# Gate and up with seven half products instead of eight in three of seven tile pairs, and the inverse transform token by token

## The chip, the cores and the metric

The program runs on one core of a Trainium2 chip. A core has TensorE (PE, with the weight load PEld shown apart), VectorE (DVE), ScalarE (ACT), GpSimd (POOL) and SyncE (SP), which here issues all DMAs. Each engine works through its instructions in the order in which the kernel emits them, and waits for the others through semaphores. The metric is the time of one execution on the device, in microseconds; lower is better.

## The reference

8192 tokens of 448 channels go through two blocks with a modulated layer norm each. The first is a Fourier transform over the tokens, a small two-layer network per frequency, and the inverse transform. The second is a gated feed-forward network of 1792 hidden channels:

```python
mod = (_silu(c) @ w_mod).reshape(c.shape[0], 6, 1, -1)
h = _layernorm(x, axis=-1) * (1 + ca) + sa
x = x + ga * _A_ref(h, A_w1, A_b1, A_w2, A_b2)
h = _layernorm(x, axis=-1) * (1 + cb) + sb
x = x + gb * (_gelu(h @ w_gate) * (h @ w_up)) @ w_down
```

Inputs and outputs are float32. The kernel keeps that accuracy by splitting operands into a high and a low float16 part and summing three products: high by high, high by low, low by high.

## The kernel before

**Stages.** A forward transform, the network on frequencies and the first half of the inverse transform take about 370 us. Then the second half of the inverse and the feed-forward network run over 32 chunks (`nch`) of 256 tokens, two blocks of 128 (called "tokens" b=0, 1 below). This loop over chunks `i` is the part that the change touches.

**Gate and up.** The 1792 hidden channels are 14 tiles of 128. They go in seven pairs t=0..6: q=0 is hidden tile t, q=1 is tile t+7. A step k=2t+q of the loop (`gate_up(i, k)`, L1096) computes gate (pr=0) and up (pr=1) of one hidden tile for the 256 tokens into one PSUM bank `pgu`: for each of the two, ten matmuls of 256 columns (L1087). The 448 channels are three whole k-tiles (each wh by high, wh by low, wl by high) and a last one of 64 channels, where high and low stand above each other. What is left of that last one, wl by high, is done for two neighbouring units (i, t) together by eight matmuls of 64 rows (L1116), when the first unit of the pair (`first_pair`, (7i+t) even) has ended its q=1. So a first unit's two outputs leave PSUM after its q=1; a second unit's leave after each q. With t even, the unit is first of its pair in even chunks and second in odd ones.

**The way out of a tile.** `gate_up_out` (L1120): ACT takes the gelu of the gate (L1123), DVE multiplies by up (L1128) into the tile `x` (three buffers), and after q=1 POOL forms four sums of 128x128 blocks (L1134 to L1137), with which `down` needs seven products instead of eight. One unit later, after odd k, `quantize` (L1139) writes the seven blocks as high (ACT, L1145) and low part (DVE, L1146).

**Down.** After k=2 of the next chunk `down(i-1)` (L1158) does seven products of 21 matmuls. The first two end in `b1` (a "pd" bank) and `b2` (a "pc" bank); ACT copies p1 (L1176) out of `b1`, the next product uses the other "pd" bank, and the one after it the bank that the p1 copy has freed.

**Beside it**, hooks prepare the chunk after next, i+2: at k=3 `split_g` and `split_v` split the transform matrix g and the values v (high on ACT L105, low on POOL L107), for both tokens; at k=6 `inverse` (six float32r matmuls, L987 to L989); at k=7 `residual` (L998, L999), at k=8 to k=10 the statistics and the inverse root, at k=11 and 12 `norm2` (L1036, L1037) into a tile of its own, at k=13 `pack_hi` (ACT, L1042) and `pack_lo` (POOL). At k=0 of the following chunk 16 DMA transposes bring the packed rows to `nt`, the moving operand of gate and up. Loads of v, g and xx (the input rows) of chunk i+2 are issued at k=0.

Of the kernel before, what the change touches and what calls it, by code (L numbers as in the profile page):

```python
# [37 lines left out]
NTT = len(PKO)  # L38
LAM = 0.01
# [6 lines left out]
def spectral_geglu(ctx, tc, x, w1, b1, w2, b2, wg, wu, wd, cvec, wmod, cf1, cs2, cmi, cgm, out):  # L46
# [272 lines left out]
    with ExitStack() as bctx:  # L319
# [359 lines left out]
        def row_scales():  # L679
# [8 lines left out]
            pow2(sk, bnd)  # L688
# [50 lines left out]
        def scales1():  # L739
# [20 lines left out]
            pow2(sw, mxa)  # L760
# [122 lines left out]
        def load_g(i):  # L883
            g = ep.tile([128, CB, 128], F32, tag="g", name="g")
            dma(g, cgm[:, i * CB : (i + 1) * CB, :])
            xx = ep.tile([128, CB, D], F32, tag="xx", name="xx")
            dma(xx, xv[:, i * CB : (i + 1) * CB, :])
            nxt.setdefault(i, {}).update({"g": g, "xx": xx})
# [22 lines left out]

        def split_g(i):
            gh = ep.tile([128, CB, 128], F32R, tag="gh", name="gh")
            gl = ep.tile([128, CB, 128], F32R, tag="gl", name="gl")
            split(gh, gl, nxt[i]["g"], el=G)
            nxt[i]["g"] = gh, gl
# [32 lines left out]
    with ExitStack() as cctx:  # L949
# [7 lines left out]

        def load_d8(t):
            load_d(t, *(cp2.tile([128, n, HC], F32, tag=f"dr{n}", name="dr", bufs=2) for n in (3, 4)))
# [8 lines left out]
        def split_v(i, cs=slice(0, D)):  # L968
            n = nxt[i]
            if "vh" not in n:  # L970
                n["vh"] = cp.tile([128, CB, D], F32R, tag="vh", name="vh")
                n["vl"] = cp.tile([128, CB, D], F32R, tag="vl", name="vl")
            for b in each(i):
                split(n["vh"][:, b, cs], n["vl"][:, b, cs], n["v"][:, b, cs], el=G)

        def inverse(i, cs=slice(0, D), tag="pc"):
            nxt[i]["ps"] = []
            for b in range(CB):
                ps = bank(tag, "pi2")[:, cs]
                if i < 3:  # L980

                    T.matmul(ps, nxt[i]["g"][:, b], nxt[i]["v"][:, b, cs], start=True, stop=True)
                    nxt[i]["ps"].append(ps)
                    continue
                vh, vl = nxt[i]["vh"], nxt[i]["vl"]
                gh, gl = nxt[i]["g"]
                T.matmul(ps, gh[:, b], vh[:, b, cs], start=True, stop=False)  # L987
                T.matmul(ps, gl[:, b], vh[:, b, cs], start=False, stop=False)  # L988
                T.matmul(ps, gh[:, b], vl[:, b, cs], start=False, stop=True)  # L989
                nxt[i]["ps"].append(ps)  # L990

        def residual(i, cs=slice(0, D)):
# [383 lines left out]
```

## Time and profile before

| | us |
|---|---|
| runs shown, median (lowest, highest) | 1941.23 (1938.67, 1942.99) |
| the profiled execution, time | 1942.27 |
| the profiled execution, span in the trace | 1940.5 |
| mean granted TensorE clock | 0.995 of full |

The page gives each engine's busy time as a share of the span; the chain that ended last names, going back from the end, what each step waited for. The windows view cuts a stretch of time out and gives the same busy times for it, with the clock and the DMA share. The timeline lists instructions in order of time, neighbours of one kind merged ("x7"): start, duration from the first start to the last end, engine, line, and in brackets how long the engine was idle before and what released it. A matmul's duration holds its way through the array, so the pace of a row of matmuls is read from start to start, not from one duration.

### The profile page before, as it was taken

How to read it: one execution, taken by the hardware profiler on the slowest of the kernel's cores; microseconds unless marked ns; L12 is line 12 of the kernel's file. 1: busy time of each engine (PE TensorE's matmuls, PEld its weight loads, DVE VectorE, ACT ScalarE, POOL GpSimd, SP SyncE). 2: the span in 40 equal slices, each digit the busy share in tenths (PEclk: the TensorE clock that was granted, in tenths of full speed). 3: DMA queues.
4: the chain of work that ended last, by engine and by line, in shares of the span. 5: the costliest groups of instructions: out<-in, count | busy, mean ns of one | idle time of the engine just before them, and what ended most of it. 6: DMA issues, size and time to landing. Idle time of an engine off the chain costs nothing.

```text
span 1940.5 us, 43566 instructions
## 1 busy us (share of the span) xinstructions
PE 1901.1 (98%) x17636; PEld 1694.6 (87%) x17636; DVE 1108.7 (57%) x2352; ACT 790.1 (41%) x1342; POOL 1157.7 (60%) x1466
## 2 busy tenths in 40 slices
PE   7899999899999999999999999999999999999998
PEld 3599999778888888888888888888888888888897
DVE  8677788786555555555555555555555555555533
ACT  5587888553333333333333333333333333333322
POOL 3157655256666666666666666666666666666644
PEclk9899999999999999999999999999999999999999
DMA  9999777541111111111111111111111111111000
GB/s 351 313 286 261 194 195 196 166 125 48 44 44 44 43 43 43 43 43 44 43 44 43 43 44 43 44 44 42 45 43 44 44 43 44 43 44 44 21 16 20
DMA packets 167330, 163.35 MB, mean 84 GB/s; under 512 B 87252, under 2 KB 145496, under 8 KB 167128
## 3 DMA queue, kind: packets, MB, share of 16 engines
q1 hardware_dynamic: 167128, 160.57, 28.3%
q8 instruction: 138, 2.26, 0.5%
q14 instruction: 64, 0.52, 0.1%
HBM read 97.44 MB, written 47.25 MB: 75 GB/s over the span
## 4 chain that ended last, share of the span: by engine, by line
PE 86%; DVE 4%; ACT 3%; issue 3%; DMA 2%; POOL 1%; SPq 1%; ACTq 0%; POOLq 0%; DVEq 0%
PE pgu L1087 53%; PE pdn L1155 8%; PE pdn L1153 8%; PE pdn L1154 8%; PE ps L202 2%; DVE y L463 2%; PE pi L989 1%; PE pi L988 1%; PE pi L987 1%; POOL yl L107 1%; DVE st L163 1%; ACT th L105 0%; DMA raw<-in_B_w_gate 0%; POOL tl L107 0%; ACT zh L376 0%
## 5 line engine op out<-in xcount | busy, mean ns | idle before, releaser
L1087 PE MATMUL pgu<-nt,wh 128*128 128x256 f16 x6272 | 834.2, 273 | 0.1
L1087 PEld LDWEIGHTS <-wh 128*128 128x128 f16 x6272 | 602.7, 98 | 98.5 <-issue 31.0
L1123 ACT ACTIVATE gel<-pgu,dg 128x256 f32<-128x256 f32 x448 | 200.3, 473 | 793.2 <-PE pgu L1087 756.1
L1087 PE MATMUL pgu<-nt,wl 128*128 128x256 f16 (+1 forms) x3584 | 501.3, 272 | 0.6 <-DVE x L1128 0.6
L1155 PE MATMUL pdn<-wd,ac 128*128 128x224 f16 x1568 | 406.1, 259 | 0.2 <-DVE ac L1146 0.2
L1153 PE MATMUL pdn<-wd,ac 128*128 128x224 f16 x1568 | 406.1, 259 | 0.0
L1154 PE MATMUL pdn<-wd,ac 128*128 128x224 f16 x1568 | 406.1, 259 | 0.0
L1134 POOL TENSOR_TENSOR x<-x 128x128 f32<-128x128 f32 x223 | 239.9, 1076 | 264.0 <-DVE x L1128 230.5
L1146 DVE SCALAR_TENSOR_TENSOR ac<-x,sa_act,ac 128x896 f16<-128x896 f32 (+1 forms) x225 | 308.2, 1370 | 81.9 <-ACT ac L1145 81.9
L1087 PEld LDWEIGHTS <-wl 128*128 128x128 f16 (+1 forms) x3584 | 297.8, 97 | 57.6 <-issue 24.4
L1128 DVE TENSOR_TENSOR x<-pgu,gel 128x256 f32<-128x256 f32 x448 | 179.6, 418 | 278.7 <-ACT gel L1123 278.0
L1145 ACT ACTIVATE ac<-x,sa_act 128x896 f16<-128x896 f32 (+1 forms) x225 | 232.9, 1035 | 46.5 <-POOL x L1137 44.5
L1190 POOL TENSOR_TENSOR o<-u,p 128x224 f32<-128x224 f32 x32 | 21.0, 657 | 291.6 <-DVE u L1189 291.6
L1135 POOL TENSOR_TENSOR x<-x 128x128 f32<-128x128 f32 x223 | 158.1, 709 | 17.5
L1155 PEld LDWEIGHTS <-ac 128*128 128x128 f16 x1568 | 153.4, 98 | 0.5 <-DVE ac L1146 0.5
L1154 PEld LDWEIGHTS <-ac 128*128 128x128 f16 x1568 | 153.4, 98 | 0.4
L1153 PEld LDWEIGHTS <-ac 128*128 128x128 f16 x1568 | 153.4, 98 | 0.4
L107 POOL TENSOR_TENSOR yl<-y,yh 128x448 fp32r<-128x448 f32 x63 | 78.9, 1252 | 75.6 <-ACT yh L105 63.0
L463 DVE SCALAR_TENSOR_TENSOR y<-pm,t 64x224 f32<-64x224 f32 x256 | 99.5, 389 | 41.3 <-ACT t L455 37.4
L1136 POOL TENSOR_TENSOR x<-x 128x128 f32<-128x128 f32 x223 | 113.0, 507 | 0.0
L1137 POOL TENSOR_TENSOR x<-x 128x128 f32<-128x128 f32 x223 | 109.2, 490 | 0.0
L107 POOL TENSOR_TENSOR tl<-tr,th 128x896 f16<-128x896 f32 x30 | 57.3, 1909 | 69.5 <-DMA tr<-td 38.2
(281 smaller groups left out, 2728.4 us busy)
## 6 DMA issues: line engine op xcount, KB each, us to landing
tr<-td SPq DMA_DIRECT2D x64, 224.0 KB, 4.3
vd<-us SPq DMA_DIRECT2D x64, 224.0 KB, 3.3
xx<-in_A_x SPq DMA_DIRECT2D x32, 448.0 KB, 3.3
v<-vd SPq DMA_DIRECT2D x63, 224.0 KB, 2.7
out<-x SPq DMA_DIRECT2D x31, 448.0 KB, 2.6
xt<-in_A_x SPq DMA_DIRECT2D x15, 896.0 KB, 14.8
td<-xt SPq DMA_DIRECT2D x48, 224.0 KB, 4.3
nt<-pk SPq DMA_TRANSPOSE x480, 2.3
```

The lines of the kernel that those rows point to most:

```text
L107: (el or V).tensor_tensor(lo, src, h, ALU.subtract)
L463: V.scalar_tensor_tensor(y[ri * 64 : ri * 64 + 64, gi], pv[si, ri], LAM, tv[si, ri], op0=ALU.add, op1=ALU.min)
L1087: T.matmul(pgu[i, t, q][:, pr * H : (pr + 1) * H], w[rows, tw, f0 : f0 + 128], nts[i][rows, tn, :], start=start, stop=stop, skip_group_che ...
L1123: S.activation(gl, ps[:, :H], AF.Gelu_apprx_tanh, scale=dg)
L1128: V.tensor_tensor(dst, ps[:, H : 2 * H].rearrange("p (b c) -> p b c", b=2), gl.rearrange("p (b c) -> p b c", b=2), ALU.mult)
L1134: e.tensor_tensor(s1, a21, a22, ALU.add)
L1135: e.tensor_tensor(s2, s1, a11, ALU.subtract)
L1145: S.activation(ac[:, 0, k], x[:, k], AF.Copy, scale=sc)
L1146: V.scalar_tensor_tensor(ac[:, 1, k], x[:, k], sc, ac[:, 0, k], op0=ALU.mult, op1=ALU.subtract)
L1153: T.matmul(ps, ac[:, 0, ka], wds[t][:, 0, kb], start=t == 0, stop=False)
L1154: T.matmul(ps, ac[:, 0, ka], wds[t][:, 1, kb], start=False, stop=False)
L1155: T.matmul(ps, ac[:, 1, ka], wds[t][:, 0, kb], start=False, stop=t == NP - 1)
```

## The change

Of the 448 channels, the first 256 (k-tiles 0 and 1) form a 2x2 grid of blocks with the two tokens on one side and, with the two hidden tiles t and t+7, on the other. Eight products of 128-blocks are replaced by seven (Winograd's form), for t = 0, 2 and 4, from chunk 3, 4 and 5 on (`SP`). Each product is gate and up times three matmuls of 128 columns. The other 192 channels stay (`rest`, from k-tile 2).

- PE: `gate_up_s1` (q=0) does six of the products, with three intermediate sums x, of which each is copied from PSUM to SBUF (`u`) by ACT before the next product is added onto it. A seventh bank user, `px` ("pc"), holds x and one product y. `gate_up_s2` (q=1) does the last product. `gate_up_out` adds u (and y) to the outputs on DVE: one 512-column add for q=0, two for q=1.
- The token side needs four sums of blocks for each chunk: `s_sums` (POOL) and `s_pack` (ACT, POOL) at k=2 for chunk i+1, and `s_transposes` at k=3, eight more DMA transposes into a longer `nt`.
- The weight side needs sums of blocks once: `sp_load`, `sp_sums`, `sp_round`, in chunks 2 to 4.
- To make room, `norm2` writes into the tile `xx`, `load_xx` moves to k=3, g and v are split one token at a time (b=0 at k=2 ahead of `down`, b=1 at k=5), and `inverse1` runs per token at k=5 and k=7, with the residual at k=6 and k=8.
- The scales for gate and up and for the normalised rows become smaller by a factor of four (`pow2(..., 13)`).

```diff
+SP = {0: 3, 2: 4, 4: 5}
...
+        def split_v(i, b):
             n = nxt[i]
+            for key, w in (("g", 128), ("v", D)):
+                h, l = (cp.tile([128, w], F32R, tag=key + p, name=key + p) for p in "hl")
+                split(h, l, n[key][:, b], el=G)
+                n[key + "2"] = h, l
...
+        def inverse1(i, b):
+            ps = bank("pc", "pi2")[:, :D]
+            (gh, gl), (vh, vl) = nxt[i]["g2"], nxt[i]["v2"]
+            T.matmul(ps, gh, vh, start=True, stop=False)
+            T.matmul(ps, gl, vh, start=False, stop=False)
+            T.matmul(ps, gh, vl, start=False, stop=True)
...
+        def s_sums(i):
+            n = nxt[i]["n"]
+            a11, a12, a21, a22 = (n[:, b, k * 128 : (k + 1) * 128] for b in range(2) for k in range(2))
+            s = nxt[i]["s"] = x8()
+            G.tensor_tensor(s[:, 0], a21, a22, ALU.add)
+            G.tensor_tensor(s[:, 1], s[:, 0], a11, ALU.subtract)
+            G.tensor_tensor(s[:, 2], a11, a21, ALU.subtract)
+            G.tensor_tensor(s[:, 3], a12, s[:, 1], ALU.subtract)
+
+        def s_pack(i):
+            s = nxt[i]["s"]
+            ps = nxt[i]["ps16"] = cp.tile([128, 4, 2, 128], F16, tag="pks", name="pks")
+            S.copy(ps[:, :, 0], s[:, :4])
+            G.tensor_tensor(ps[:, :, 1], s[:, :4], ps[:, :, 0], ALU.subtract)
...
+        def rest(i, t, q, pr, first_pair, j0):
+            seq = [(wh, j, j) for j in range(j0, 4)] + [(wh, j, j + 5) for j in range(j0, 3)] + [(wl, j, j) for j in range(j0, 3)]
+            for j, (w, tw, tn) in enumerate(seq):
+                last = not first_pair and not j0 and j == len(seq) - 1
+                gu(i, t, q, pr, w, full, tw, tn, first_pair and pr == 0 and j == 0, last)
...
+        def sp_product(i, t, o, ka, kb, start=False, stop=False):
...
+            for pr in range(2):
+                for n, (l, la) in enumerate(((0, 0), (0, 1), (1, 0))):
+                    T.matmul(
+                        o[:, pr],
+                        weight(pr, l),
+                        act(la),
...
+        def gate_up_s1(i, t, first_pair):
+            pv = bank("pc", "px").rearrange("p (x r c) -> p x r c", x=2, r=2)
+            sums["px"] = pv
+            x, u = pv[:, 0], sums["u"]
+            sp_product(i, t, x, 0, 0, start=True)
+            sp_product(i, t, pv[:, 1], 3, 3)
+            S.copy(u[:, :, 0], x)
+            rest(i, t, 0, 0, first_pair, 2)
+            sp_product(i, t, x, 4, 6)
+            S.copy(u[:, :, 1], x)
+            rest(i, t, 0, 1, first_pair, 2)
+            o = outs(i, t, 0)
+            sp_product(i, t, o[:, :, 0], 1, 1, stop=not first_pair)
+            sp_product(i, t, x, 5, 4, stop=True)
+            S.copy(u[:, :, 2], x)
+            sp_product(i, t, o[:, :, 1], 2, 5, stop=not first_pair)
+
+        def gate_up_s2(i, t, first_pair):
+            for pr in range(2):
+                rest(i, t, 1, pr, first_pair, 2)
+            sp_product(i, t, outs(i, t, 1)[:, :, 0], 6, 2, stop=not first_pair)
...
         def gate_up_out(i, t, q):
+            if seven(i, t):
+                u, o = sums["u"], outs(i, t, q)
+                if q == 0:
+                    V.tensor_tensor(o, o, u[:, :, 0::2], ALU.add)
+                else:
+                    y = sums["px"][:, 1].unsqueeze(2).broadcast_to([128, 2, 2, 128])
+                    V.tensor_tensor(u[:, :, 1:3], y, u[:, :, 1:3], ALU.add)
+                    V.tensor_tensor(o, o, u[:, :, 1:3], ALU.add)
...
-            3: [(2, split_g), (2, split_v)],
-            6: [(2, inverse)],
-            7: [(2, residual)],
-            8: [(2, stats2)],
+            3: [(2, load_xx), (1, s_transposes)],
+            5: [(2, inverse1, 0), (2, split_v, 1)],
+            6: [(2, residual, slice(0, D), [0])],
+            7: [(2, inverse1, 1)],
+            8: [(2, residual, slice(0, D), [1]), (2, stats2)],
...
+                if k == 2 and 3 <= i + 1 < nch:
+                    s_sums(i + 1)
+                    s_pack(i + 1)
+                if k == (4, 3, 2)[min(i, 2)] and 3 <= i + 2 < nch:
+                    split_v(i + 2, 0)
+                for fn, *args in sp_work.pop(i * NFT + k, []):
+                    fn(*args)
                 if k == 2 and i > 0:
                     down(i - 1)
```

`quantize` after odd k, `pack_hi` and `pack_lo` at k=13 and `down` at k=2 keep their places in the loop.

More of the change, by code (lines that the diff above doesn't have):

```diff
@@ L995, in residual @@
             x1 = x1t[i][:, :, cs]
-            for b in range(CB):
+            for b in bs:
                 e = V if i < 3 else G
@@ L1103, in gate_up @@
                         pgu[(*divmod(u, NP), qq)] = bank(tag, "pgu")
[L1104 to L1107 removed]
+            if seven(i, t):
+                (gate_up_s1, gate_up_s2)[q](i, t, first_pair)
+            else:
+                for pr in range(2):
+                    rest(i, t, q, pr, first_pair, 0)
             if not first_pair:
@@ L1268, in spectral_geglu @@
         pack_lo(0)
+        load_g(1)
         for t0 in range(0, 7, 2):
```

121 lines of the change are left out of this document (86 added, 35 removed).

## The prediction

> **What bounds the kernel now.** I read the page's busy shares first, then the chain that ended last, then two neighbouring chunks in the windows view.
>
> ```profile
> PE 1901.1 (98%) x17636; PEld 1694.6 (87%) x17636; DVE 1108.7 (57%) x2352; ACT 790.1 (41%) x1342; POOL 1157.7 (60%) x1466
> ...
> PE 86%; DVE 4%; ACT 3%; issue 3%; DMA 2%; POOL 1%; SPq 1%; ACTq 0%; POOLq 0%; DVEq 0%
> ```
>
> ```profile
> 861.62:910.24 48.62, 48.62 (x467) 43.27 (x465) 25.85 (x52) 15.45 (x26) 31.75 (x42) 1.00 0.16 43
> 910.24:958.12 47.88, 47.88 (x460) 43.08 (x458) 24.49 (x50) 15.97 (x27) 30.50 (x40) 1.00 0.16 44
> ```
>
> The windows are chunk 10 (even) and chunk 11 (odd), cut where their first tile starts on PE. The columns are length, then PE, PEld, DVE, ACT, POOL busy, clock, DMA. PE is busy in all of both, so in a chunk the time is PE's own work: less PE work is worth its full length, and any wait that PE gets is paid in full. ACT works 16 of 48 us, so it has time; whether it has it at the right moment is the question of this change.
>
> **The matmuls.** I write k for a half tile (k = 2t+q), T0 for the moment when PE starts the half tile spoken of.
>
> ```profile
> 861.62 0.93 PE L1087 MATMUL pgu<-nt,wh 128*128 128x256 f16 x7
> 862.38 0.49 PE L1087 MATMUL pgu<-nt,wl 128*128 128x256 f16 x3
> 862.71 0.93 PE L1087 MATMUL pgu<-nt,wh 128*128 128x256 f16 x7
> ```
>
> ```profile
> 250.84 0.22 PE L368 MATMUL ps<-s,th 128*112 128x128 f16 x1
> ...
> 252.13 0.22 PE L370 MATMUL ps<-s,tl 128*112 128x128 f16 x1
> ```
>
> ```profile
> 416.62 0.40 PE L1069 MATMUL ptr<-ident,pk 128*128 128x128 f16 x4
> ```
>
> Ten matmuls of 256 columns take 1.09 us from start to start, 0.109 each. The second fence holds the first and the last of 24 matmuls of 128 columns, each with a weight load of its own (112 columns): 1.29/23 = 0.056 us. The third has the change's shape exactly, but only four of it: (0.40 - 0.22)/3 = 0.060. A seven-product unit drops 24 matmuls of 256 columns (2.62 us) and adds 7 x 2 x 3 = 42 of 128 (2.35 at 0.056, 2.52 at 0.060). It saves 0.26 to 0.10 us; I take 0.26, from the longer run. There are 29 + 28 + 27 = 84 such units: 22 us, and no more.
>
> One rule speaks against even that. The Trainium skill, "TensorE: Matmul & The Clock Gate", section "Back-to-back issue gap", gives about 81 ns for a sustained stream of weight load and 128-column matmul; the rows above, 56 ns over 24 pairs, do not agree, and by 81 ns a unit would cost 0.78 us more than before instead of 0.26 less.
>
> **The first copy.** `gate_up_s1` puts product 1 and the product kept as y on PE (12 x 0.056), then four matmuls of 256 (0.44): after 1.11 us PE wants to add the next product onto x, and must not before ACT has copied x to u. The copy is queued on ACT behind everything emitted for the half tile before.
>
> ```profile
> 885.09 0.93 PE L1087 MATMUL pgu<-nt,wh 128*128 128x256 f16 x7
> ...
> 885.29 0.47 ACT L1123 ACTIVATE gel<-pgu,dg 128x256 f32<-128x256 f32 x1 [9.89 <-PE pgu L1087]
> 885.66 1.03 ACT L1145 ACTIVATE ac<-x,sa_act 128x896 f16<-128x896 f32 x1
> ...
> 933.71 0.94 PE L1087 MATMUL pgu<-nt,wh 128*128 128x256 f16 x7
> ...
> 934.43 1.04 ACT L1145 ACTIVATE ac<-x,sa_act 128x896 f16<-128x896 f32 x1
> ```
>
> These are k=4 of chunk 10 and of chunk 11, PE's start and ACT's work. The gelu of k=3 can only run once PE has ended k=3, that is after T0, and the quantize of an odd half tile stands right behind it. It ends 886.69 - 885.09 = 1.60 us after T0 in the even chunk, 1.76 in the odd one. None of this is touched by the change. The copy itself, 256 columns out of PSUM, is not in the trace; its nearest rows are these two:
>
> ```profile
> L1123 ACT ACTIVATE gel<-pgu,dg 128x256 f32<-128x256 f32 x448 | 200.3, 473 | 793.2 <-PE pgu L1087 756.1
> ...
> L1182 ACT COPY p<-pdn 128x224 f32<-128x224 f32 x32 | 11.1, 346 | 62.5 <-PE pdn L1155 62.5
> ```
>
> Between 0.35 and 0.47; I take 0.37, since it is a copy, and 0.05 for the signal. PE stands still for 1.60 + 0.42 - 1.11 = **0.91 us** (even) and **1.07** (odd). That alone is more than the three savings of a chunk, 0.78. The second copy has ACT to itself, with 0.77 us of PE work over it, so I cost it at nothing; without that cover it is about 0.6 us.
>
> At k=0 the pack of another chunk stands in the queue too.
>
> ```profile
> 863.53 1.04 ACT L1145 ACTIVATE ac<-x,sa_act 128x896 f16<-128x896 f32 x1 [1.24 <-POOL x L1137]
> 864.74 0.94 ACT L1042 CAST pk<-n 128x896 f16<-128x896 f32 x1 [0.16 <-DVE n L1037]
> ...
> 912.68 0.92 ACT L1042 CAST pk<-n 128x896 f16<-128x896 f32 x1
> ```
>
> T0 is 861.62 and 910.24. ACT is free 4.06 us after T0 in the even chunk (865.68), 3.36 in the odd one. The waits are 4.06 + 0.42 - 1.11 = **3.37** and **2.67**. If POOL and DVE were never behind, the quantize would end at 1.6 and the pack at 2.55, and the wait would still be 1.86.
>
> **The longer way out of a tile.** Three DVE adds of 512 columns are new in front of the gelus. By the rows here, 448 columns from PSUM take 0.60 and 256 take 0.42; I take 0.66 for 512.
>
> ```profile
> L1128 DVE TENSOR_TENSOR x<-pgu,gel 128x256 f32<-128x256 f32 x448 | 179.6, 418 | 278.7 <-ACT gel L1123 278.0
> ...
> L998 DVE TENSOR_TENSOR x<-pi,ga_r 128x448 f32<-128x448 f32 (+1 forms) x66 | 37.3, 601 | 0.0
> ```
>
> DVE and ACT now go add, gelu, product, add, add, gelu, product: 3 x 0.66 + 2 x 0.47 + 2 x 0.42 = 3.8, with signals 4.2 us. In even chunks this starts at the end of the tile (first of its pair), in odd ones at the end of q=0, 1.2 us earlier (q=1 is now eight matmuls of 256 and six of 128): 4.2 and 3.0 us after the tile's end. Then POOL's four sums follow.
>
> ```profile
> 869.95 1.30 POOL L1134 TENSOR_TENSOR x<-x 128x128 f32<-128x128 f32 x1
> 871.33 0.46 POOL L1135 TENSOR_TENSOR x<-x 128x128 f32<-128x128 f32 x1
> 871.74 0.46 POOL L1136 TENSOR_TENSOR x<-x 128x128 f32<-128x128 f32 x1
> 872.15 0.46 POOL L1137 TENSOR_TENSOR x<-x 128x128 f32<-128x128 f32 x1
> ```
>
> 2.66 us, so a tile's values are ready 6.9 (even) or 5.7 us (odd) after it. Two things are now queued behind them.
>
> **Down.** At k=2 the change emits, ahead of `down`, `s_sums` on POOL (behind the sums of t=0), and on ACT the pack copy that waits for it and two split copies.
>
> ```profile
> 868.82 0.26 PE L1153 MATMUL pdn<-wd,ac 128*128 128x224 f16 x1
> ...
> 872.76 0.35 ACT L1176 COPY p<-pdn 128x224 f32<-128x224 f32 x1 [3.26 <-PE pdn L1155]
> 875.06 0.35 ACT L1182 COPY p<-pdn 128x224 f32<-128x224 f32 x1 [1.95 <-PE pdn L1155]
> ```
>
> The p1 copy (L1176) frees the bank that the third product of `down` needs. That product would start about 0.2 us before the p4 copy, at 874.86, so the p1 copy may begin up to 874.45, which is 5.63 us after `down` starts, 7.82 after the end of k=1. Now ahead of it: 6.9 for t=0, four sums of 0.46, a 512-column cast (0.62, between 0.57 for 448 and 0.94 for 896) and casts of 128 and 448 columns (0.9): 10.2 us. PE waits **2.4**; odd: 9.0, **1.2**.
>
> ```profile
> L105 ACT CAST yh<-y 128x448 fp32r<-128x448 f32 x64 | 36.2, 566 | 40.4 <-DVE y L463 40.2 <-DVE y L475 0.2
> ...
> L105 ACT CAST vh<-v 128x896 fp32r<-128x896 f32 x29 | 27.3, 941 | 0.0
> ```
>
> **The second token's inverse.** Its split is emitted at k=5, so its POOL half stands behind the sums of t=2; its matmuls come two half tiles later.
>
> ```profile
> 889.90 0.72 POOL L107 TENSOR_TENSOR gl<-g,gh 128x256 fp32r<-128x256 f32 x1
> 890.59 2.10 POOL L107 TENSOR_TENSOR vl<-v,vh 128x896 fp32r<-128x896 f32 x1
> ...
> 893.04 0.36 PE L987 MATMUL pi<-vh,gh 128*128 128x448 f32 x1
> ...
> 893.66 0.94 PE L1087 MATMUL pgu<-nt,wh 128*128 128x256 f16 x7
> ...
> 909.70 0.61 PE L1087 MATMUL pgu<-nt,wl 64*128 64x256 f16 x8
> ```
>
> Before, these stand ahead of the sums of t=2 (their first starts when vl is done). Half of each is about 0.4 and 1.15, so they are ready 6.9 + 1.55 = 8.4 us after k=5. PE asks for them after one token's inverse (0.62) and two half tiles (4.4), and for the last piece 0.4 later, at 5.4: PE loses **3.0** in the even chunk. In the odd one k=7 also holds the eight shared half matmuls (0.6): 5.7 + 1.55 = 7.2 against 6.0, **1.15**. By then ACT has done the quantize in front of k=8, so I cost the copy of t=4 at nothing; if this wait is absent, that copy costs about 0.3.
>
> **The sum.** Even 0.91 + 3.37 + 2.4 + 3.0 = 9.7; odd 1.07 + 2.67 + 1.2 + 1.15 = 6.1; mean 7.9, less 0.8 saved: 7.1 a chunk. Chunks 5 to 31: 27 x 7.1 = 192. Chunks 2 to 4, with part of it, add about 11; the last two, without splits, take off 6. Together +197. The profiled execution took 1942.3 us (span 1940.5; the median of the runs is 1941.2), so **2140 us**. The loads, sums and rounding of the new weights, the eight more transposes and the added POOL sums (about 5 us a chunk beside 31) I cost at nothing beyond the waits above: SP, ACT and POOL have 15 us and more free in a chunk. Uncovered, each is one to two us a chunk.
>
> **The rivals.**
> *Only the first copies hold PE* (0.22): POOL and DVE catch up while PE waits, and `down` and the inverse stay covered. Even 3.37 + 0.91 + 0.3, odd 2.67 + 1.07 + 0.4, mean 4.4 less 0.8: 3.6 x 27 + 6 = +103, 2045 us; with the pack on time (1.86) about 2010. For it: POOL and DVE idle a third of a chunk.
> *The clock drops as well* (0.12).
>
> ```profile
> 404.00:408.00 4.00, 1.73 (x15) 1.28 (x13) 3.96 (x6) 1.91 (x4) 1.15 (x2) 0.89 0.00 0
> 408.00:412.00 4.00, 4.00 (x29) 3.12 (x28) 4.00 (x5) 3.09 (x5) 4.00 (x4) 0.68 0.62 178
> ```
>
> PE was busy for 1.73 of the first 4 us, a pause of up to 2.3; the clock then ran at half for some 3.4 us (it lacks 0.11 + 0.32 of 4 us each, twice that at one half). The waits at k=0 are longer. One drop costs 1.7 us: one a chunk gives 2190, two 2235. The Trainium skill, same page, "Part 1: The HAM clock gate", has idle windows of 3.4 us that run freely, which would let some such pauses pass; the trace's one drop neither proves nor denies it.
> *The copies are on time* (0.07), the faster side: if ACT were done with quantize and pack by T0 + 0.69, PE would never wait and 84 x 0.26 gives 1920 us. For it only that ACT is 59% idle; against it, the rows above, with 1.60 at the least.
> *They cancel* (0.03): waits of 0.26 a unit, 1942.
> *128-column matmuls at 81 ns* (0.02): 84 x 0.78 = 66 in place of -22, with somewhat shorter waits, about 2200; the 56 ns row is against it.
>
> **How the numbers follow.** Forecast 0.54, 2080 to 2225 (each wait 30% shorter, or up to 40% longer as backlog is handed from chunk to chunk). The range reaches down through the first rival: 2010 to 2225. What a measurement can tell from no change is about 0.2%: faster 0.07, same 0.03, slower 0.90.
>
> **What would show it.** PE idle ahead of the product on x, released by ACT's copy, about 1 us at k=4 and 3 us at k=0; PE idle in `down` released by the p1 copy; PE idle at the second token's inverse released by POOL. Starts 0.056 us apart in the products show the saving. A PE without idle time there makes the forecast wrong, and so does ACT running the copy ahead of the quantize.

## The result, and the profile after

| | before | after |
|---|---|---|
| median of 4 runs each, us (lowest, highest) | 1939.95 (1937.19, 1942.99) | 2296.61 (2293.79, 2297.65) |
| profiled execution, us (span) | 1942.27 (1940.5) | 2297.60 (2295.8) |
| mean granted TensorE clock | 0.995 | 0.953 |

The changed kernel is slower by a ratio of 1.184, interval 1.181 to 1.186: 355 us in the two profiled executions, where the forecast was 2140, 198 more. The direction was right and the amount too small; the time lies above the range.

The page of the changed kernel, busy shares and chain:

```profile
PE 1992.5 (87%) x19148; PEld 1751.4 (76%) x19148; DVE 1257.0 (55%) x2616; ACT 896.7 (39%) x1693; POOL 1266.9 (55%) x1693
...
PE 39%; DVE 23%; POOL 16%; ACT 12%; issue 7%; DMA 2%; SPq 0%; POOLq 0%; ACTq 0%; DVEq 0%
```

PE carried 86% of the chain before and carries 39% now: the end is set by relays between DVE, POOL and ACT. No engine is full, DVE and POOL are at 55%. What is missing is not capacity, but a result at the moment when PE asks for it.

The windows view, chunk 8 (even) and chunk 9 (odd), cut where their first tile starts, columns as before:

```profile
842.80:905.33 62.53, 52.27 (x522) 45.53 (x519) 30.83 (x62) 19.43 (x39) 34.58 (x48) 0.95 0.14 38
905.33:963.54 58.21, 51.19 (x512) 45.19 (x512) 29.73 (x59) 19.28 (x38) 34.30 (x47) 0.94 0.16 41
```

Ten and seven us of a chunk are now without a matmul, and the clock is at 0.95 and 0.94 where it was 1.00. Who PE waited for, in the waits view of the whole run (total us, times, longest):

```profile
PE px L1191 <- ACT dr L1210: 156.5, 58, 8.5
PE pdn L1292 <- ACT p L1315: 33.4, 25, 1.9
PE pgu L1113 <- DVE x L1267: 25.5, 26, 7.2
PE pi L992 <- POOL gl L109: 25.2, 26, 1.6
PE pi L993 <- POOL vl L109: 16.7, 27, 0.6
```

Rows one, two, four and five are the places that the prediction named: the first copy, the p1 copy in `down`, the second token's inverse. Row three it did not name: the eight shared half matmuls (L1113) write into a bank that DVE has not read yet. Counted in the trace over 22 steady chunks (from `down` of chunk 6 to that of chunk 28), as PE idle per chunk:

| place | predicted, even / odd | idle found, even / odd |
|---|---|---|
| first copy, k=0 | 3.37 / 2.67 | 5.00 / 4.23 |
| first copy, k=4 | 0.91 / 1.07 | 0.65 / 0.85 |
| fourth product of `down`, which needs p1's bank (the prediction calls it the third) | 2.4 / 1.2 | 1.89 / 0.73 in 7 of 11 |
| second token's inverse | 3.0 / 1.15 | 2.45 / 0.96 |
| shared half matmuls | none | 0.23 / 0.97 |

The prediction counted from start to start, the table has only the time in which the array is empty. One wait is about 0.17 us longer by the first measure (k=4: from 936.65 to 937.78 less one matmul of 0.11 is 1.02, the row says 0.85). There are about six waits a chunk, so the mean of 8.85 idle is 9.9 in the prediction's measure, against its 7.9. A steady chunk (the mean of an even and an odd one) takes 60.3 us instead of 48.25, that is 12.1 more.

**The wait at k=0.** The timeline of PE, chunk 9, and then that of ACT, POOL and DVE over the same time, DVE's from further back:

```profile
905.33 0.29 PE L1191 MATMUL px<-nt,wh 128*128 128x128 f16 x2
...
906.01 0.49 PE L1113 MATMUL pgu<-nt,wh 128*128 128x256 f16 x3
906.33 0.27 PE L1113 MATMUL pgu<-nt,wl 128*128 128x256 f16 x1
910.83 0.80 PE L1191 MATMUL px<-nt,dr 128*128 128x128 f16 x6 [4.23 <-ACT dr L1210]
```

```profile
908.64 1.04 ACT L1284 ACTIVATE ac<-x,sa_act 128x896 f16<-128x896 f32 x1 [2.57 <-POOL x L1276]
909.59 0.92 ACT L1045 CAST pk<-xx 128x896 f16<-128x896 f32 x1
910.42 0.36 ACT L1210 COPY dr<-px 128x256 f32<-128x256 f32 x1
```

```profile
904.93 1.29 POOL L1273 TENSOR_TENSOR x<-x 128x128 f32<-128x128 f32 x1 [2.41 <-DVE x L1267]
906.31 0.71 POOL L1274 TENSOR_TENSOR x<-x 128x128 f32<-128x128 f32 x1
906.99 0.83 POOL L1275 TENSOR_TENSOR x<-x 128x128 f32<-128x128 f32 x1
907.78 0.83 POOL L1276 TENSOR_TENSOR x<-x 128x128 f32<-128x128 f32 x1
```

```profile
894.91 0.63 DVE L1011 BATCH_NORM_STATS2 cst<-x 128x6 f32<-128x448 f32 x1 [2.23 <-POOL x L1003]
895.45 0.30 DVE L1014 BATCH_NORM_AGGREGATE cmv<-cst 128x2 f32<-128x6 f32 x2
895.67 0.68 DVE L1255 TENSOR_TENSOR pgu<-pgu,dr 128x512 f32<-128x512 f32 x1
...
898.01 0.70 DVE L1259 TENSOR_TENSOR pgu<-pgu,dr 128x512 f32<-128x512 f32 x1
...
901.31 0.42 DVE L118 TENSOR_SCALAR rcve<-cmv 128x2 f32<-128x2 f32 x1
...
904.44 0.42 DVE L1267 TENSOR_TENSOR x<-pgu,gel 128x256 f32<-128x256 f32 x1
```

Read it from the bottom. T0 is 905.33. DVE's adds for t=4 (L1255, L1259) stand behind the statistics of k=8, and these wait 2.23 us for POOL's residual sum. The inverse root (from L118 on) and the product of t=5 at 904.44 come behind all of that. Then POOL needs 3.7 us for its sums, and the quantize starts 3.31 us after T0. Behind it stand the pack and, at 910.42, the copy that PE wants. In the kernel before (chunk 11, T0 910.24) the quantize started 1.50 after T0, and the prediction took that time over:

```profile
911.74 1.04 ACT L1145 ACTIVATE ac<-x,sa_act 128x896 f16<-128x896 f32 x1 [0.66 <-POOL x L1137]
```

**The clock.** Windows of four us around this pause (clock is the third number from the end):

```profile
904.00:908.00 4.00, 2.29 (x27) 1.40 (x25) 3.90 (x8) 0.84 (x2) 2.99 (x4) 1.00 0.00 0
908.00:912.00 4.00, 1.17 (x9) 1.04 (x9) 2.83 (x5) 2.47 (x4) 2.70 (x4) 0.68 0.04 8
912.00:916.00 4.00, 4.00 (x30) 3.39 (x29) 0.95 (x2) 0.89 (x3) 2.76 (x5) 0.50 0.11 21
916.00:920.00 4.00, 4.00 (x42) 3.78 (x41) 2.79 (x5) 1.40 (x2) 1.24 (x2) 0.97 0.12 25
```

Twice what the clock lacks of full is the time at half: 2 x 4 x (0.32 + 0.50 + 0.03) = 6.8 us. Over the 22 chunks it is 6.36 us a chunk, of which 1.35 lies in the pauses themselves; in the rest the products start 0.107 us apart instead of 0.056, so it costs PE half of 5.0, that is 2.5 us a chunk.

**The sum.** 9.9 of waits and 2.5 of clock, less 0.8 saved, is 11.6 of the 12.1 measured; 0.5 was not placed. Over the whole run: up to `down` of chunk 0 the new kernel is 4 us ahead, the five chunks from there lose 63, the 24 after them 290, the end 6.

### The profile page after: what moved, and what is told of

Same layout as the page of the kernel before. It is cut to its first block, busy times and chain, and to the rows that moved or that the text cites. A ratio compares the mean times of both kernels' runs of the same rounds, so it can differ in the third digit from the quotient of the medians.

```text
span 2295.8 us, 48046 instructions
## 1 busy us (share of the span) xinstructions
PE 1992.5 (87%) x19148; PEld 1751.4 (76%) x19148; DVE 1257.0 (55%) x2616; ACT 896.7 (39%) x1693; POOL 1266.9 (55%) x1693
## 4 chain that ended last, share of the span: by engine, by line
PE 39%; DVE 23%; POOL 16%; ACT 12%; issue 7%; DMA 2%; SPq 0%; POOLq 0%; ACTq 0%; DVEq 0%
PE pgu L1113 11%; PE pdn L1292 5%; PE pdn L1294 4%; PE pdn L1293 4%; PE px L1191 4%; POOL x L1274 4%; ACT gel L1262 4%; DVE x L1267 4%; PE pgu L1191 3%; ACT ac L1284 2%; DVE pgu L1259 2%; DVE pgu L1255 2%; POOL x L1273 2%; DVE ac L1285 2%; POOL x L1003 2%
## 5 line engine op out<-in xcount | busy, mean ns | idle before, releaser
L1113 PE MATMUL pgu<-nt,wh 128*128 128x256 f16 x4928 | 708.6, 279 | 1.1 <-DVE x L1267 1.0
L1113 PEld LDWEIGHTS <-wh 128*128 128x128 f16 x4928 | 475.2, 100 | 73.6 <-issue 20.1
L1273 POOL TENSOR_TENSOR x<-x 128x128 f32<-128x128 f32 x223 | 178.6, 801 | 559.7 <-DVE x L1267 555.5
L1113 PE MATMUL pgu<-nt,wl 128*128 128x256 f16 (+1 forms) x2912 | 447.9, 276 | 24.9 <-DVE x L1267 24.5
L1285 DVE SCALAR_TENSOR_TENSOR ac<-x,sa_act,ac 128x896 f16<-128x896 f32 (+1 forms) x225 | 278.8, 1239 | 94.5 <-ACT ac L1284 94.5
L1113 PEld LDWEIGHTS <-wl 128*128 128x128 f16 (+1 forms) x2912 | 235.9, 98 | 81.2 <-issue 48.5
L1191 PEld LDWEIGHTS <-dr 128*128 128x128 f16 x1512 | 119.7, 114 | 172.3 <-issue 170.8
L1191 PE MATMUL px<-nt,dr 128*128 128x128 f16 x1008 | 103.8, 252 | 157.0 <-ACT dr L1210 156.5
L1274 POOL TENSOR_TENSOR x<-x 128x128 f32<-128x128 f32 x223 | 205.9, 923 | 17.5
L1255 DVE TENSOR_TENSOR pgu<-pgu,dr 128x512 f32<-128x512 f32 x84 | 58.6, 697 | 215.4 <-PE pgu L1113 124.5
L1191 PEld LDWEIGHTS <-wh 128*128 128x128 f16 x1344 | 118.2, 104 | 25.4 <-ACT wh L1170 6.9
```

The costliest lines, as they stand in the source:

```text
L1113: T.matmul(pgu[i, t, q][:, pr * H : (pr + 1) * H], w[rows, tw, f0 : f0 + 128], nts[i][rows, tn, :], start=start, stop=stop, skip_group_che ...
L1191: T.matmul(o[:, pr], weight(pr, l), act(la), start=start and pr == 0 and n == 0, stop=stop and n == 2, skip_group_check=True,)
L1255: V.tensor_tensor(o, o, u[:, :, 0::2], ALU.add)
L1273: e.tensor_tensor(s1, a21, a22, ALU.add)
L1274: e.tensor_tensor(s2, s1, a11, ALU.subtract)
L1285: V.scalar_tensor_tensor(ac[:, 1, k], x[:, k], sc, ac[:, 0, k], op0=ALU.mult, op1=ALU.subtract)
```

## The experiments

All times are medians, compared with runs of the kernel before on the same chip. The first four keep all work and test the reading of the k=0 wait.

**The pack behind the copy.** If the pack is what lengthens the wait at k=0, moving it must shorten the wait by its own length.

```diff
         hooks = {
-            0: [(1, transposes_dma)],
+            0: [(1, pack_hi), (1, pack_lo), (1, transposes_dma)],
...
-            13: [(2, pack_hi), (2, pack_lo)],
```

> The changed kernel with the pack of the chunk ahead (its ACT cast and POOL part) emitted after k=0 instead of after k=13, so that it no longer stands before the first copy of x at k=0. Theory (the copy waits for its turn on ACT, and the quantize ahead of the pack is itself late because POOL's sums of t=5 are late): the wait at k=0 shrinks only by the pack's own 0.9 to 1.1 us, the clock still drops after it, time about 2265 us. Rival (the pack is what holds PE): the wait of about 4.8 us and the half clock behind it go, about 2070 us.

2280.98 us, ratio 1.174 (1.172 to 1.176). The wait at k=0 became 3.89 and 3.39, about 1 us shorter, all others stayed. A chunk takes 59.3 us. The run became 16 us shorter, half of what the theory gave, and the rival falls: the pack was one link, and the smaller one.

**The quantize behind the copies.** Where a seven-product tile comes next, the quantize is emitted after that tile's three copies, and before its way out.

```diff
             if seven(i, t):
                 (gate_up_s1, gate_up_s2)[q](i, t, first_pair)
+                while held:
+                    quantize(*held.pop())
...
+                    if (n % NFT) % 2 == 0 and seven(n // NFT, n % NFT // 2):
+                        held.append(j)
+                    else:
+                        quantize(*j)
```

> The changed kernel with the quantize that stands ahead of a seven-product tile emitted behind its three copies instead. Theory: the waits of about 0.9 us at k=4 go, those at k=0 shrink by only some 0.4 us because the pack, released by DVE's norm at about the same moment, still stands in the queue; about 2258 us. Rival (the quantize is what holds PE at k=0 too): about 2050 us.

2416.31 us, ratio 1.245 (1.243 to 1.247): 120 us slower than the change, where both theories had it faster. The wait at k=4 is gone, as intended. But the quantize has a half on DVE as well (L1285 in the changed kernel, L1287 here), and DVE too takes its work in order. DVE's timeline of this kernel:

```profile
1105.20 1.15 DVE L1287 SCALAR_TENSOR_TENSOR ac<-x,sa_act,ac 128x896 f16<-128x896 f32 x1 [7.56 <-ACT ac L1286]
1106.27 0.69 DVE L1257 TENSOR_TENSOR pgu<-pgu,dr 128x512 f32<-128x512 f32 x1
...
1111.28 0.70 DVE L1261 TENSOR_TENSOR pgu<-pgu,dr 128x512 f32<-128x512 f32 x1
```

DVE stands still for 7.56 us, until ACT has done the three copies and the quantize; only then come the adds of the tile that PE has left. So every bank is freed later. The waits view of PE in this kernel, 900 to 1700 us (13 chunks of the changed kernel, 12 of this):

```profile
PE px L1191 <- ACT dr L1210: 41.5, 12, 3.8
PE pgu L1113 <- DVE x L1269: 33.8, 25, 3.0
PE pdn L1294 <- ACT p L1317: 22.2, 12, 1.9
PE pi L992 <- POOL gl L109: 21.0, 13, 1.6
```

In the changed kernel the same stretch has 74.4, 8.2, 14.2 and 12.0 us in these four places: the first fell, the other three rose. The clock was at half for 9.8 us a chunk instead of 6.4.

**Both moves.** Pack and quantize both behind the copies, with the two edits above.

> Both moves together. Theory: at k=0 and k=4 only the gelu stands before the copy, PE waits under 0.5 us, never 2 us at one place at the start of a chunk, and the clock stays full: (4.8 + 0.9 + 3.2) us in 28 chunks less, about 2045 us, more than the two single moves together. Rival (the late chains on DVE and POOL hold PE whatever ACT's order is, the wait only moves to the shared half matmuls, down and the inverse): 2150 to 2250 us.

2320.70 us, ratio 1.196 (1.193 to 1.198), above both expectations. The waits for the first copy are gone at k=0 and k=4 alike, and the kernel is slower than the change. In the waits view of 900 to 1700 us the row of the first copy (L1191, ACT) is missing, and these lead:

```profile
PE pgu L1113 <- DVE x L1269: 34.8, 25, 3.0
PE pdn L1294 <- ACT p L1317: 24.5, 13, 1.9
PE pi L992 <- POOL gl L109: 21.0, 13, 1.6
```

So clearing ACT's queue ahead of the copies does not bring the time back, and the rival's reading, "the wait only moves", fits. But this run does not separate the two: the moved quantize also holds DVE, as in the run before, so part of the new waits is made by the edit. That the wait at k=0 had given DVE and POOL time to catch up is a reading, not shown. The next kernels, which leave work out, separate them.

**The clock by itself.** The pause at k=0 is filled with 40 matmuls of 256 columns with zero weights, which add zero to a bank that is open anyway.

```diff
+            if t == 0:
+                for _ in range(40):
+                    T.matmul(pgu[i, t, 0][:, :H], zt, nts[i][:, 2, :], start=False, stop=False, skip_group_check=True)
             sp_product(i, t, x, 4, 6)
```

> The changed kernel with 40 extra matmuls of 256 columns with weights of zero at k=0, ahead of the second product on x, while PE would be idle (they add zero to the output). Theory (the pause of 4 to 5 us at k=0 makes the clock drop to half for 6.8 us, 3.2 us lost in each chunk): no half clock in the loop, about 93 us less, 2205 us. Rival (the clock drops for another reason, or half clock costs nothing because PE would wait anyway): 2290 to 2310 us.

2267.71 us, ratio 1.169 (1.167 to 1.170). The time at half clock fell from 6.36 to 1.55 us a chunk, so the pause is what lowers the clock. A chunk became 1.5 us shorter (58.8), the run 29. The gain expected, 93 us, was far too large. Without the part of the half clock that lies in the pauses, 2.5 us a chunk before and 0.73 now, 1.8 were to be had, and the odd chunks' `down` gave part of that back (its wait rose from 0.73 in 7 of 11 to 1.02 in every one).

**One half of the new work at a time.** The next kernels leave work out, to price it. In the first the three copies out of x are left out (`u` stays zero), the adds remain.

```diff
-            S.copy(u[:, :, 0], x)
...
-            S.copy(u[:, :, 1], x)
...
-            S.copy(u[:, :, 2], x)
```

> The changed kernel without ACT's three copies of x in each seven-product tile (u is set to zero once and the adds read that; the sums P1+P6 and so on are left out of the output). PE then waits for nothing on x. Theory now (after e2 and e5: the lateness is in DVE's and POOL's queues, and PE's waits only move): the pauses at k=0 and k=4 go, those at the shared half matmuls, down and the inverse stay or grow, about 2250 us, between 2150 and 2330. Rival (the theory of the prediction: the copies' turn on ACT is most of the loss): about 2045 us.

2149.78 us, ratio 1.108 (1.106 to 1.110): 147 us below the change, at the lowest time that the theory gave and 105 us above the rival's. So the copies' turn on ACT is not most of the loss. PE's waits are those of `down` (1.90 and some 0.4 to 0.8 more), the inverse and the half matmuls.

In the second the three DVE adds of `gate_up_out` are left out and the copies remain.

```diff
-                if q == 0:
-                    V.tensor_tensor(o, o, u[:, :, 0::2], ALU.add)
-                else:
-                    y = sums["px"][:, 1].unsqueeze(2).broadcast_to([128, 2, 2, 128])
-                    V.tensor_tensor(u[:, :, 1:3], y, u[:, :, 1:3], ALU.add)
-                    V.tensor_tensor(o, o, u[:, :, 1:3], ALU.add)
```

> The changed kernel without DVE's three adds of 512 columns in each seven-product tile (what they add is left out of the output), copies kept. Theory now: a tile's way out is 2 us shorter, so the wait at k=0 falls from 4.8 to about 3 us as worked out from the trace of before, down to 1.4, the inverse to under 1, the wait at k=4 stays at 0.9; with half clock behind k=0 about 2150 us. Rival (the adds run beside other work and cost nothing): about 2290 us.

2071.19 us, ratio 1.068 (1.066 to 1.070): 225 us below the change, more than either side expected. The waits view of 900 to 1700 us has one row:

```profile
PE px L1191 <- ACT dr L1210: 47.5, 31, 2.9
```

The waits of `down`, of the inverse and of the half matmuls are all gone, so they came from the adds. At k=0 the wait is 2.87 (even) and 1.73 (odd) instead of 5.00 and 4.23; the prediction, from times of the kernel before, had 3.37 and 2.67. With DVE on time its reading would have been somewhat too long, not too short.

**Neither copies nor adds.** Both are left out, the pack of the block sums goes behind `down`, and the first inverse and second split to k=4. What remains is PE's own work, the loads and the preparation of the weights.

```diff
-            5: [(2, inverse1, 0), (2, split_v, 1)],
+            4: [(2, inverse1, 0), (2, split_v, 1)],
...
-                    s_pack(i + 1)
...
                 if k == 2 and i > 0:
                     down(i - 1)
+                    if 3 <= i + 1 < nch:
+                        s_pack(i + 1)
```

> The changed kernel without the copies and without the adds (both left out of the output), with the pack of the block sums emitted behind down and the second token's split at k=4, so that what is left is PE's own work. The prediction's saving, 84 x 0.26 us: 1920 us, and 1930 to 1940 with small waits left. Rival (the products of 128 columns cost more than 0.060 us each, or other waits of 2 us and more remain in each chunk): 1980 us and more.

1953.03 us, ratio 1.006 (1.005 to 1.008). The time lies between the two expectations. A steady chunk takes 47.45 us, 0.80 less than before, and PE has no idle time in it: three units of 0.26, as worked out. But four chunks at the start are long. The windows view, from `down` of chunk 0 to that of chunk 4, first of the kernel before, then of this one:

```profile
434.30:627.30 193.00, 193.00 (x1846) 172.68 (x1844) 105.90 (x223) 63.78 (x105) 125.82 (x163) 1.00 0.17 46
```

```profile
433.90:658.80 224.90, 200.38 (x1919) 176.35 (x1917) 108.19 (x231) 67.97 (x123) 144.86 (x204) 0.96 0.18 48
```

32 us are lost there. The waits view from 440 to 700 us shows the relay:

```profile
ACT dr L1171 <- POOL o L1161: 16.2, 6, 5.7
...
POOL o L1158 <- DMA o<-in_B_w_gate: 11.0, 3, 6.2
...
PE px L1192 <- ACT wh L1171: 6.7, 1, 6.7
```

POOL's sums of the new weights wait for the load that was issued three half tiles earlier, ACT's rounding (`sp_round`) waits for POOL, and whatever stands behind the rounding on ACT waits with it.

**The preparation spread out.** As the last one, with one of gate and up per chunk, its sums five and its rounding six half tiles behind the load.

```diff
-SP = {0: 3, 2: 4, 4: 5}
+SP = {0: 4, 2: 6, 4: 8}
...
-                k = (i - 1) * NFT + 5 + 4 * pr
+                k = (i - 2 + pr) * NFT + 5
                 sp_work[k] = sp_work.get(k, []) + [(sp_load, t, pr)]
-                sp_work[k + 3] = [(sp_sums, t, pr)]
-                sp_work[k + 4] = [(sp_round, t, pr)]
+                sp_work[k + 5] = [(sp_sums, t, pr)]
+                sp_work[k + 6] = [(sp_round, t, pr)]
```

Also xx of chunk 3 is loaded ahead of chunk 2's transposes.

> The kernel of e9 (no copies, no adds, both left out of the output) with the preparation of the new weights spread: gate and up in different chunks, the sums five and the rounding six half tiles after the load, first use in chunks 4, 6 and 8 instead of 3, 4 and 5, and the input rows of chunk 3 loaded ahead of chunk 2's transposes. e9 lost 33 us in chunks 1 to 5 and nothing after. Theory (ACT and DVE stand still for weights that DMA and POOL have not brought, and the tiles' way out stands behind them): most of the 33 us goes, 1922 to 1932 us. Rival (the loss is in the first use or the start of the loop itself): 1945 us and more.

1922.52 us, ratio 0.991 (0.989 to 0.992), as expected: PE's saving is real, 19 us, and the placing of the preparation (with that one load of xx) costs 30 us, once. From `down` of chunk 0 to that of chunk 4:

```profile
434.40:632.80 198.40, 196.27 (x1883) 174.29 (x1882) 109.08 (x229) 67.72 (x122) 138.80 (x196) 0.98 0.19 51
```

5 us instead of 32 are lost there.

**Copies alone, adds alone.** The first is the kernel without copies and adds, with the copies put back and pack and quantize behind them (the edits shown); the second has the adds put back instead.

> No adds (left out of the output), copies kept, with pack and quantize emitted behind the copies, the block sums' pack behind down, second token's split at k=4: e9 plus the three copies. Theory (a copy costs PE only by what stands before it on ACT): 1953 to 1968 us. Rival (each copy is a round trip that PE pays wherever it stands): 2000 us and more.

1982.20 us, ratio 1.021 (1.020 to 1.023). 29 us more than without them, between the two expectations; a chunk takes 48.16 us, 0.71 more, with no idle time of over 0.05 us on PE: most of it is three products on x a chunk that start some 0.19 us late, too short to show as idle. In the kernel without adds above, the same copies stood behind pack and quantize, and a steady chunk took 51.28 us. What stands ahead of a copy on ACT decides its price, and here nothing long does.

> No copies (the sums P1+P6 and so on left out of the output), adds kept, the block sums' pack behind down, second token's split at k=4: e9 plus the three adds. Theory (the adds lengthen the way out of a tile, and DVE's queue hands that on, to the shared half matmuls above all): waits of 1 to 2 us a chunk, 1980 to 2020 us. Rival 1 (with down and the inverse out of the way the adds are covered): 1955 us. Rival 2 (the adds cost their 9 us a chunk wherever they stand): 2150 us.

2045.62 us, ratio 1.054 (1.052 to 1.056). 93 us more, above what was expected; 51.15 us a chunk, 3.7 more, with the clock full. Its waits, 900 to 1700 us:

```profile
PE pgu L1113 <- DVE x L1265: 22.3, 24, 1.1
PE px L1192 <- DVE x L1002: 13.0, 8, 1.9
PE pdn L1292 <- DVE ac L1283: 9.5, 16, 0.8
```

Nearly everything that PE waits for here is DVE's (a fourth row, ACT's, has 1.8 us): banks read late, the residual's product that has to empty the bank which x needs, the quantize's low half.

Alone, copies and adds cost 29 + 93 = 122 us; together, in the order of the change, 2296.6 - 1953.0 = 344. The other 222 us belong to neither alone: they come from the two together and from their order (the small moves of the block sums' pack, the split and the inverse among it).

**All the work, in another order.** If the order is the cost, an order exists that avoids it. Three kernels with nothing left out. The first moves each quantize to a half tile without copies, and pack, block sums' pack, residual and statistics behind the copies and `down`:

```diff
-            0: [(1, transposes_dma)],
+            1: [(1, pack_hi), (1, pack_lo), (1, transposes_dma)],
...
+            at = {0: [(i - 1, 5)], 5: [(i, 1)], 9: [(i, 2), (i, 3)], 12: [(i, 4)]}
```

> The whole change, with everything that is not on a tile's way out emitted where it stands before no copy, add or gelu of a seven-product tile: quantize of t=0 behind down, t=2 and 3 at k=9, t=4 at k=12, t=5 behind k=0, t=6 between the two halves of t=0; pack at k=1; the pack of the block sums behind down; second token's split at k=4, residual, statistics, inverse root and norm at k=9 to 13. Theory now (queue order on three engines, not the amount of work): waits under 1 us a chunk, clock full, about 1950 us. Rival (the longer way out itself is too long for four banks): 2050 us and more.

2180.70 us, ratio 1.124 (1.121 to 1.128). Better than the change by 116 us, and in the rival's range, though not for the rival's reason alone: the longest waits were again a matter of place, since the next product on x at k=8 waited for the residual in both kinds of chunk, 2.7 and 3.0 us. The second puts some high halves of a quantize between two gelus, the residual's product (DVE) at k=5 and k=8 with its sum on POOL apart, and block sums' pack and first split inside `down`; it also spreads the preparation. Its core:

```diff
+                if q:
+                    his(i, k)
                 gate_up_out(i, t, q)
...
+            if 3 <= i + 2 < nch:
+                s_pack(i + 2)
+            if i >= 1 and i + 3 < nch:
+                split_v(i + 3, 0)
             p7 = product(i, bank("pd", "pdn"), 5, 4)
...
-            6: [(2, residual, slice(0, D), [0])],
+            5: [(2, res_mul, 0)],
+            6: [(2, res_add, 0)],
```

> The whole change, complete, with the spread preparation of e10, and the queues rebuilt: quantize of t=5 and the pack behind the copies of k=0, the ACT halves of the quantizes of t=6, 1 and 3 between the two gelus of a seven-product tile, t=2 at k=8, t=4 at k=12, t=0 behind down; block sums' pack and first token's split inside down; residual's product at k=5, its sum at k=6. Theory (order alone): waits under 0.7 us a chunk, 1930 to 1955 us. Rival (the longer way out does not fit into four banks and one px): 2030 us and more.

2054.42 us, ratio 1.058 (1.056 to 1.061). Again the rival's time. Steady chunks take about 50.6 us with the clock full, but chunks 2 to 8 take 55 to 60: in the stretch from 660 to 720 us ACT's rounding waited 9.4 us for POOL's sums, and these 7.8 us for their load, which was issued behind the transposes. The third loads the weights two half tiles earlier and rounds them eight half tiles after the load, moves two of the output's products ahead of the second and third product on x, so that they cover the copies, and lets the first three products of `down` begin without t=5 and t=6:

```diff
             rest(i, t, 0, 0, first_pair, 2)
+            o = outs(i, t, 0)
+            sp_product(i, t, o[:, :, 0], 1, 1)
             sp_product(i, t, x, 4, 6)
             S.copy(u[:, :, 1], x)
             rest(i, t, 0, 1, first_pair, 2)
-            o = outs(i, t, 0)
-            sp_product(i, t, o[:, :, 0], 1, 1, stop=not first_pair)
+            sp_product(i, t, o[:, :, 1], 2, 5, stop=not first_pair)
             sp_product(i, t, x, 5, 4, stop=True)
             S.copy(u[:, :, 2], x)
-            sp_product(i, t, o[:, :, 1], 2, 5, stop=not first_pair)
...
-            product(i, b1, 0, 0, range(NP - 1))
-            product(i, b2, 1, 1, range(NP - 1))
+            product(i, b1, 0, 0, range(5))
+            product(i, b2, 1, 1, range(5))
+            product(i, b3, 2, 5, range(5))
```

> The whole change, complete. g2 with: the new weights loaded at k=3 ahead of the transposes and rounded eight half tiles later; the quantize of t=6 finished before the second output of t=0, that of t=3 at k=10; in the tile, the first output product moved ahead of the first copied sum's use and the second one ahead of the last (1.44 us of cover in place of 1.11); in down, the first three products run over t=0 to 4 first and take t=5 and 6 after that. Theory (the loss is order and lateness, not the amount of work on ACT, DVE and POOL): the pauses of 5 to 9 us in chunks 2 to 8 go and those of 1.2 us at down and 0.55 at the half matmuls too, a chunk takes 48 to 49.5 us, 1945 to 1985 us. Rival (the adds cost about 3.5 us a chunk as in e12 however they are placed): a chunk of 50.5 us and more, 2010 us and more.

1994.11 us, ratio 1.028 (1.026 to 1.029): with the change's whole work, 302 us below it, and still 53 above the kernel before. A chunk takes 50.4 us, nearly the rival's 50.5; its time came out lower, since the start is as it should be. Its waits of 900 to 1700 us, about 16 chunks:

```profile
PE pgu L1121 <- DVE x L1279: 19.3, 25, 1.1
PE pdn L1324 <- ACT p L1348: 8.7, 16, 0.8
PE pdn L1326 <- DVE ac L1300: 7.1, 8, 0.9
```

The first copies hold nothing any more. Three quarters of what is left (26.4 of 35.1 us) is waited for from DVE; the rest is the p1 copy on ACT. Against the kernel without copies and adds but with spread preparation, they cost 1994.1 - 1922.5 = 72 us in this order. No order tried beats the kernel before, and whether one could was not settled.

## Why the prediction was right in direction and wrong in size

**The matmuls: right.** In the fence of k=0 above the twelve product matmuls run from 905.33 to 906.01, 0.057 each, and the kernel without copies and adds saves 0.80 us a chunk against 0.78. The rival at 81 ns each falls, and with it, for this stream, the figure of the Trainium skill's "TensorE: Matmul & The Clock Gate", "Back-to-back issue gap": no run here shows it.

**The copy, and the wait at k=4: right.** The copy took 0.37 us. Start to start PE lost 0.82 and 1.02 against 0.91 and 1.07. ACT's timeline at k=4 of chunk 9 shows the queue as it was worked out:

```profile
935.70 0.84 ACT L1262 ACTIVATE gel<-pgu,dg 128x256 f32<-128x256 f32 x2 [10.51 <-PE pgu L1113]
936.42 1.04 ACT L1284 ACTIVATE ac<-x,sa_act 128x896 f16<-128x896 f32 x1
937.36 0.37 ACT L1210 COPY dr<-px 128x256 f32<-128x256 f32 x1
```

**The adds, `down` and the inverse: right in place and cause, nearly in size.** An add took 0.697 us against 0.66. The kernel without the adds has none of these waits. The product of `down` that waits for p1's bank is the fourth, not the third as the prediction says; the time that it worked with, 874.86, is that of the fourth. `down` came out shorter than worked out (1.89 for 2.4, and 0.73 in 7 of 11 for 1.2), the inverse as it was: 2.45 idle in three pieces, with 0.17 for each 2.95 against 3.0.

**The wait at k=0: the step that failed first.** "ACT is free 4.06 us after T0 in the even chunk (865.68), 3.36 in the odd one" is a time of the kernel before, and the sum took it as if nothing ahead of it moved. But the change lengthens what stands ahead: the adds of t=4, the residual behind POOL's sums, and with them the statistics, the products and sums of t=5. The quantize starts 1.8 us later against T0 (3.31 for 1.50). That is 1.8 us a chunk, start to start (5.17 and 4.40 for 3.37 and 2.67). The prediction used its own longer way out for `down` and for the inverse, and not for the quantize at k=0. The run without the adds shows that they did it: there the wait is 2.87 and 1.73.

**The clock: taken as a rival that excludes the forecast, where it adds to it.** It had a chance of 0.12. The forecast had waits of 2.67 and 3.37 us at k=0, and the pause that it priced, 2.27 us, had lowered the clock. It was not "the trace's one drop": ahead of the loop the trace of the kernel before has a pause of 4.27 us (at 75.46) with 10.24 us at half behind it, one of 6.25 (at 371.56) with 6.83, and one of 2.63 (at 19.76) with none. So a drop could cost more than 1.7, and a pause of under 3 us could go either way. In the changed kernel the clock dropped at nearly every k=0, for 6.83 us in most cases, twice the stretch from which one drop was priced at 1.7. It costs 2.5 us a chunk. The filling run shows the cause, and that less comes back than is lost.

**The half matmuls: not foreseen,** 0.6 us a chunk. They write into the next unit's banks, which the longer way out frees late.

**The preparation: costed at nothing, and 30 us.** "SP, ACT and POOL have 15 us and more free in a chunk" is true and answers the wrong question: a rounding that waits 5.7 us for sums and a load blocks the queue behind it for that time, on an engine that is mostly idle. The 30 us are those of the kernel without copies and adds; no run spreads the preparation alone in the change itself.

Together: the 24 steady chunks lost 12.1 us each where 7.1 was forecast, 120 us more, of which 1.8 (k=0), 2.5 (clock) and 0.6 (half matmuls) are named above, less 0.5 for `down`. The five chunks before them lost 63, where their share of the sum was some 20, and the preparation's 30 us would be most of that difference. The waits by themselves, 9.9 for 7.9, are 25% longer, inside the 40% that the range allowed; with the clock's 2.5 us in 24 chunks (60 us) and the long start on top, the time left the range. So the steps that failed are three: the k=0 wait read from times of the old kernel, the clock kept out of the sum, and the preparation put at nothing.

**The first rival,** that only the first copies hold PE (2045), falls: without any copy the kernel still took 2149.78, with the waits of `down`, of the inverse and of the half matmuls in it. **The rival that the copies are on time** (1920) came true only where nothing else was left: 1922.5 without copies and adds.

## What to carry to other kernels

Work added to an engine that is half idle is priced first by what stands ahead of it and behind it in that engine's queue (here 344 us in one order and 72 in another), and the lateness has to be followed on to the next stage and the next chunk, not read from the time at which things ended in the old kernel. Before a wait is moved, list what is queued behind the moved instruction on each engine that it uses; two halves of one step on ACT and DVE moved together cost 120 us here. When PE is the bound, a long pause on it (here 4.2 to 5.0 us) has two prices, its length and the clock after it.

## What the runs showed of the hardware that was not expected

- In the 22 steady chunks of the runs, where the clock dropped, the half clock came in stretches of 3.41, 6.83 and, once (the quantize behind the copies), 10.24 us, whatever ended the pause. The Trainium skill, "TensorE: Matmul & The Clock Gate", "HAM oscillation — how this bites in real kernels", warns of pauses over about 3.4 us. The 4.2 to 5.0 us pauses of the change agree.
- Single long pauses are not all that counts. In the kernel without copies, the clock dropped in every other chunk at the second token's inverse, where PE stands still three times within some four us and never for more than 1.62 (0.18 + 1.62 + 0.57 idle in the mean). In the kernel without adds, single pauses of 2.87 us, one in each even chunk, were followed by a single drop in 22 chunks. The page's rule of one long pause does not cover the first of these, nor the drop after 2.27 us in the kernel before; what decides was not tried.
